# Stage A of batch 1 in the first FFN group, W_out cast on GpSimd, and Y of batch 0 two slots sooner: a Fourier filter with a squared-ReLU FFN on one Trainium2 core

## The chip, the cores and the metric

One core of a Trainium2 chip. The metric is device time in microseconds (us) of one execution; a median of several executions is quoted. TensorE is the matmul engine, VectorE, ScalarE and GpSimd the others, SyncE issues the DMAs. In the profile they are PE (its weight loads PEld), DVE, ACT, POOL and SP.

## The reference

```python
X = np.fft.rfft(x, axis=1)                  # x: 8 x 3008 x 256
Y = X * (filt_r + 1j * filt_i)[None]
y = np.fft.irfft(Y, n=3008, axis=1)
h = np.maximum(y.reshape(24064, 256) @ w_in, 0.0)      # d_ff = 2048
return (h * h @ w_out).astype(np.float32)
```

The FFT is factored: stage A (sums over 47 rows), a re-layout through DRAM (u written as dU, read back as ut), stage B, the product with the filter, stage P, a second re-layout (ze to dZ to zt), and stage Y, which makes the input yt of the FFN. Everything runs as fp16 matmuls.

## The kernel before

The FFN runs in groups of 512 tokens, eight *slots* each. A slot holds one first-layer unit of the group, one second-layer unit of the group before, and pieces of the FFT of a later batch:

```python
for s in range((NG + 1) * SLOTS):
    g, k = divmod(s, SLOTS)
    if g < NG:
        ffn_g1(g, k)            # 4 matmuls + Relu on ScalarE
    run(work, s, 0)             # FFT pieces, place 0
    if g > 0:
        ffn_g2(g - 1, k)        # 8 matmuls
    run(work, s, 1)             # FFT pieces, place 1
    if g > 0:
        ffn_out(g - 1, k)
    if g < NG:
        ffn_sq(g, k)            # square of h on VectorE
```

Batch 0 is transformed ahead of slot 0, as are three quarters of stage A of batch 1. The first group therefore has no second layer beside it. The end of that prologue, and the plan of batch 1 (its slot numbers are those of the loop):

```python
    read_z(0, 0)
    load_wout(0)
    read_z(0, 1)
    load_wout(1)
    for c in (0, 2, 1):
        chunk_a(1, c)           # stage A of batch 1, three of four chunks
    for c in (0, 2, 1):
        write_u(1, c)
    for n in range(4):
        unit_y(0, n)
    prologue[0] = False
    for c in range(2, 4):
        read_z(0, c)            # third and fourth zt tile of batch 0
...
            for n in range(4, 16):
                put(n if n < 8 else n + 2 if n < 12 else 2 * n - 7, n % 2, unit_y, 0, n)
            for k in range(4):
                put((4, 5, 7, 7)[k], 1, cast_wout, k, nc.vector)
        t0 = 2 if b == 1 else 6
        for a in range(12 if b == 1 else 0, 16):
            put(t0 + a // 2, a % 2, unit_a, b, a)
```

Stage A and stage Y units share two PSUM buffers (`psF`). The fp32 W_out lies in a buffer of the ring of h (`h2`), so the first Relu of group 1 has to wait for the last cast of W_out. Y units with odd n are evicted by VectorE in the first group, those with even n by ScalarE.

## Time and profile before

| | |
|---|---|
| time, first three runs | 793.39, 793.43, 793.74 us |
| profiled execution | span 791.9 us, granted clock 1.0 |
| TensorE busy | 778.9 us, 98% |
| Relu of slot 0 to Relu of slot 14 | 50.96 to 73.45: **22.49 us** |

The last row is my yardstick. One row of ScalarE's timeline (start, duration, engine, line, operation, operands, then the idle time before it and what ended it):

```profile
73.45 1.02 ACT L566 ACTIVATE h<-psH 128x1024 f16<-128x1024 f32 x1 [0.89 <-PE psH L562]
```

The rest of the profile before stands in the prediction.

### The profile page before, as it was taken

To read this page: it belongs to the slowest core of one execution; us is meant where nothing else is said; L and a number is where in the kernel's file an instruction comes from. 1 tells how busy PE (TensorE), PEld (TensorE's weight loads), DVE (VectorE), ACT (ScalarE), POOL (GpSimd) and SP (SyncE) were. 2 spreads that over 40 slices of the span, in tenths; PEclk is the share of its full clock that TensorE was granted. 3 is DMA by queue.
4 is the path that set the end of the run, shared out by engine and by line. 5 is a ranking of instruction groups with operands and counts; after the bars stand their busy time and mean duration, and the time that the engine had idled before them with its cause. 6 is when DMAs were issued, how large, how long until landed. Compare 5 with 4: busy or idle time off the path is not lost.

```text
span 791.9 us, 14822 instructions
## 1 busy us (share of the span) xinstructions
PE 778.9 (98%) x6102; PEld 552.5 (70%) x6102; DVE 550.3 (69%) x897; ACT 557.4 (70%) x711; POOL 23.6 (3%) x36
## 2 busy tenths in 40 slices
PE   8989999999999999999999999999999999999998
PEld 5746667667676777867777676776767677676666
DVE  6866994579755897559965699556995579553342
ACT  3976776777777777767776777676777777776664
POOL 3800000000000000000000000000000000000000
PEclk9999999999999999999999999999999999999999
DMA  9994554346814557154562555424563332611111
GB/s 363 368 260 153 146 157 111 93 135 167 205 42 112 167 155 180 48 173 135 132 167 65 163 147 155 112 80 148 159 180 86 97 133 66 147 40 41 41 41 54
DMA packets 88571, 107.32 MB, mean 136 GB/s; under 512 B 6336, under 2 KB 79040, under 8 KB 84288
## 3 DMA queue, kind: packets, MB, share of 16 engines
q1 hardware_dynamic: 88296, 106.19, 46.5%
q8 instruction: 48, 0.79, 0.4%
q10 hardware_dynamic: 144, 0.18, 0.1%
q14 instruction: 19, 0.16, 0.1%
q0 software_dynamic: 64, 0.00, 0.0%
HBM read 58.12 MB, written 48.23 MB: 134 GB/s over the span
## 4 chain that ended last, share of the span: by engine, by line
PE 89%; DVE 6%; DMA 3%; ACT 1%; SPq 0%; issue 0%; DVEq 0%; ACTq 0%
PE psO L579 40%; PE psH L562 38%; PE psA L361 3%; PE psY L532 2%; PE psB L445 2%; DMA f<-in_filt_i_dram 2%; PE psP L496 2%; DVE prod L453 2%; DVE h L570 1%; DMA wout<-in_moe_w_out_dram 1%; PE psf L287 1%; PE psf L290 1%; DVE yf L467 0%; ACT sF L298 0%; DVE yf L461 0%; ACT h L566 0%
## 5 line engine op out<-in xcount | busy, mean ns | idle before, releaser
L566 ACT ACTIVATE h<-psH 128x1024 f16<-128x1024 f32 x376 | 384.9, 1024 | 189.3 <-PE psH L562 186.7
L579 PE MATMUL psO<-sWout,h 128*128 128x256 f16 x3008 | 388.9, 272 | 0.6 <-DVE h L570 0.6
L562 PE MATMUL psH<-yt,sWin 128*128 128x512 f16 (+7 forms) x1728 | 386.9, 351 | 1.6 <-DVE yt L541 0.7
L579 PEld LDWEIGHTS <-h 128*128 128x128 f16 x3008 | 290.6, 98 | 79.1 <-DVE h L570 0.9
L570 DVE TENSOR_TENSOR h<-h 128x1024 f16<-128x1024 f16 x376 | 252.6, 685 | 104.7 <-ACT h L566 104.5
L562 PEld LDWEIGHTS <-sWin 128*128 128x128 f16 x1728 | 159.5, 98 | 101.7 <-issue 3.3
L453 DVE TENSOR_TENSOR prod<-psB,sF 128x1024 f16<-128x1024 f32 x84 | 102.3, 1218 | 2.8 <-PE psB L445 2.8
L541 DVE CAST yt<-psY 128x376 f16<-128x376 f32 x62 | 34.0, 549 | 59.4 <-PE psY L532 59.4
L367 DVE CAST u<-psA 96x512 f16<-96x512 f32 x50 | 34.3, 687 | 47.3 <-PE psA L361 45.1
L498 ACT CAST ze<-psP 128x512 f16<-128x512 f32 x84 | 49.1, 585 | 17.2 <-PE psP L496 14.7
L590 ACT COPY ost<-psO 128x512 f32<-128x512 f32 (+1 forms) x96 | 55.8, 581 | 6.8 <-PE psO L579 5.3
L532 PE MATMUL psY<-sC,zt 112*128 112x94 f16 x512 | 42.4, 205 | 1.4 <-DMA zt<-dZ 1.4
L532 PEld LDWEIGHTS <-zt 112*128 112x128 f16 x512 | 35.1, 98 | 11.6 <-issue 1.6
L467 DVE TENSOR_TENSOR yf<-prod,yf 128x512 f16<-128x512 f16 x84 | 35.7, 425 | 2.9
L361 PE MATMUL psA<-x,sC 94*96 94x512 f16 x96 | 36.6, 382 | 0.0
L445 PE MATMUL psB<-ut,sSB 128*128 128x256 f16 x192 | 36.5, 273 | 0.0
L496 PE MATMUL psP<-yf,sSP 128*128 128x256 f16 x168 | 32.1, 272 | 0.5 <-DVE prod L453 0.3
L539 ACT CAST yt<-psY 128x376 f16<-128x376 f32 x66 | 30.9, 468 | 2.0 <-issue 1.7
L445 PEld LDWEIGHTS <-sSB 128*128 128x128 f16 x192 | 18.5, 98 | 19.5
L340 DVE CAST x<-x 94x2048 f16<-94x2048 f32 x24 | 29.2, 1216 | 0.0
L365 ACT CAST u<-psA 96x512 f16<-96x512 f32 x50 | 28.6, 572 | 0.0
L460 DVE COPY yf<-prod 64x512 f16<-64x512 f16 x84 | 24.3, 289 | 2.9
(65 smaller groups left out, 253.2 us busy)
## 6 DMA issues: line engine op xcount, KB each, us to landing
x<-in_x_dram SPq DMA_DIRECT2D x20, 768.0 KB
zt<-dZ SPq DMA_DIRECT2D x64, 192.0 KB
dU<-u SPq DMA_DIRECT2D x28, 384.0 KB
dZ<-ze SPq DMA_DIRECT2D x28, 384.0 KB
out_dram<-ost SPq DMA_DIRECT2D x66, 128.0 KB
out_dram<-ost SPq DMA_DIRECT2D x31, 256.0 KB
ut<-dU SPq DMA_DIRECT2D x7, 1024.0 KB
xw<-in_x_dram SPq DMA_DIRECT2D x6, 1024.0 KB
```

Source lines behind the costliest of these rows:

```text
L361: nc.tensor.matmul(ps[0:96, :], sSA, x16s[(b, c)][:, m, :], start=True, stop=True)
L445: nc.tensor.matmul(ps[:, i * D:(i + 1) * D], sSB[:, 2 * p + i, :], uts[b][:, 2 * p + i, :], start=True, stop=True)
L453: nc.vector.tensor_mul(out=prod, in0=ps.rearrange("p (a d) -> p a d", d=D).unsqueeze(1).to_broadcast([128, 2, 2, D]), in1=sF[:, :, 2 * p:2 ...
L467: nc.vector.tensor_add(out=yf, in0=prod[:, 0], in1=yf)
L496: nc.tensor.matmul(ps[:, i * D:(i + 1) * D], sSP[:, 2 * p + i, :], yf[:, i, :], start=True, stop=True)
L498: nc.scalar.copy(out=zes[(b, c)][:, 2 * i6:2 * i6 + 2, :], in_=ps.rearrange("p (a d) -> p a d", d=D))
L532: nc.tensor.matmul(ps[:, 94 * jj:94 * jj + 94], zt[:, 4 * (g % 2) + jj, dt * 128:(dt + 1) * 128], sSY, start=True, stop=True)
L562: nc.tensor.matmul(ps[:, i, o:o + n], sWin[:, dt, jt * 128:(jt + 1) * 128], yts[b][:, dt, r:r + n], start=(dt == 0), stop=(dt == 1))
L566: nc.scalar.activation(out=h2[:, 2 * s:2 * s + 2, :], in_=ps, func=AF.Relu)
L570: nc.vector.tensor_mul(out=v, in0=v, in1=v)
L579: nc.tensor.matmul(pso[g][:, t % 2, :], h2s[g][:, jt, t * 128:(t + 1) * 128], sWout[:, jt, :], start=(jt == 0), stop=(jt == NJT - 1))
L590: nc.scalar.copy(out=ost[:, h0:h0 + step, :], in_=pso[g][:, h0:h0 + step, :])
```

## The change

The intent: TensorE idles in group 0, so stage A can move there out of the full slots 8 and 9. Its u cannot take a u buffer (the three are still being written out), so it takes one of x. VectorE evicts it, and to make room there W_out is cast on GpSimd. Y of batch 0 follows two slots sooner.

```diff
         if i == 0:
-            us[(b, c)] = p_u.tile([96, 8, D], F16, tag="u", name=f"u_{b}_{c}")
+            pool, tag = (p_x16, "x16") if b == 1 else (p_u, "u")
+            us[(b, c)] = pool.tile([96, 8, D], F16, tag=tag, name=f"u_{b}_{c}")
...
-        if a % 2 == 0:
+        if a % 2 == 0 and b > 1:
             nc.scalar.copy(out=o, in_=pv)
...
-                put(n if n < 8 else n + 2 if n < 12 else 2 * n - 7, n % 2, unit_y, 0, n)
+                put(n if n < 12 else 2 * n - 7, n % 2, unit_y, 0, n)
             for k in range(4):
-                put((4, 5, 7, 7)[k], 1, cast_wout, k, nc.vector)
-        t0 = 2 if b == 1 else 6
+                put((1, 2, 4, 5)[k], 1, cast_wout, k, nc.gpsimd)
+        t0 = 6
         for a in range(12 if b == 1 else 0, 16):
-            put(t0 + a // 2, a % 2, unit_a, b, a)
+            put(a - 11 if b == 1 else t0 + a // 2, a % 2, unit_a, b, a)
```

## The prediction

> **What bounds the kernel now.** I read the page first: busy shares, then the chain that ended last.
>
> ```profile
> PE 778.9 (98%) x6102; PEld 552.5 (70%) x6102; DVE 550.3 (69%) x897; ACT 557.4 (70%) x711; POOL 23.6 (3%) x36
> PE 89%; DVE 6%; DMA 3%; ACT 1%; SPq 0%; issue 0%; DVEq 0%; ACTq 0%
> ```
>
> TensorE sets the time, and its work is the same after the change: the same matmuls in another order. Only TensorE's idle time can be won or lost, 791.9 - 778.9 = 13 us in all. The change touches the first FFN group (slots 0 to 7, about 51 to 61 us) and slots 8 to 13, so I next read the timeline of each engine there. TensorE:
>
> ```profile
> 57.60 1.02 PE L562 MATMUL psH<-yt,sWin 128*128 128x512 f16 x4
> 58.46 0.33 PE L532 MATMUL psY<-sC,zt 112*128 112x94 f16 x4
> 58.88 0.38 PE L562 MATMUL psH<-yt,sWin 128*128 128x512 f16 x1
> 59.76 0.81 PE L562 MATMUL psH<-yt,sWin 128*128 128x512 f16 x3 [0.50 <-DVE yt L541]
> 60.40 0.38 PE L356 MATMUL psA<-xw,sC 128*96 128x512 f16 x1
> ```
>
> A first-layer unit (4 matmuls, L562) takes 0.87 us of issue, yet slots 6 and 7 start 1.29 us apart: the group has no second layer yet, and TensorE waits for buffers that ScalarE and VectorE empty. The unit of slot 8 waits for the last Y eviction (L541). The stage A unit after it, at 60.40, belongs to what the change moves. ScalarE and VectorE:
>
> ```profile
> 50.96 1.94 ACT L566 ACTIVATE h<-psH 128x1024 f16<-128x1024 f32 x2 [1.31 <-DMA wout<-in_moe_w_out_dram]
> 58.67 1.08 ACT L566 ACTIVATE h<-psH 128x1024 f16<-128x1024 f32 x1
> 60.98 1.02 ACT L566 ACTIVATE h<-psH 128x1024 f16<-128x1024 f32 x1 [1.23 <-DMA zt<-dZ]
> ...
> 57.96 1.28 DVE L570 TENSOR_TENSOR h<-h 128x1024 f16<-128x1024 f16 x2
> 59.16 0.54 DVE L541 CAST yt<-psY 128x376 f16<-128x376 f32 x1
> 59.62 1.28 DVE L333 CAST sWout<-wout 128x1024 f16<-128x1024 f32 x2
> ```
>
> Eight Relus start from 50.96 to 58.67. A Relu lasts 1.02 us and the next can start 0.92 later (1.94 - 1.02); VectorE's squares and casts come 0.60 apart (1.28 - 0.68). The Relu at 60.98 is named as waiting for a DMA, but the last W_out cast ended at 59.62 + 1.28 = 60.90: the h buffer of group 1 is the one that holds the fp32 W_out, so I put this wait down to the cast.
>
> From 60.40 TensorE has no gap until 80.75. Thereafter VectorE is nearly continuous too, with 0.2 to 0.6 us gaps on TensorE. So a gain or loss made before slot 8 should be carried unchanged to the end.
>
> **What the Trainium skill says.** "SBUF — State Buffer", section "Who interferes with whom": VectorE and GpSimd share one port pair; a VectorE cast in a 2-port mode, or a tensor_tensor with two SBUF inputs, and a GpSimd instruction that reads SBUF exclude each other for the whole instruction. The trace agrees for casts:
>
> ```profile
> 20.49 1.04 POOL L222 CAST f<-f 128x1024 f16<-128x1024 f32 x1 [2.37 <-DMA f<-in_filt_i_dram]
> 20.56 1.51 DVE L222 CAST f<-f 128x1024 f16<-128x1024 f32 x1 [0.26 <-DMA f<-in_filt_i_dram]
> ```
>
> VectorE's cast usually takes 0.68 us; here it ended 0.54 after GpSimd's. For the squares (L570, two SBUF inputs) no overlap with GpSimd occurs in this trace, so that half of the statement is unseen here. "DMA: Bandwidth & Descriptors", section "Queues, rings and completion order": each DMA engine consumes a ring's descriptors in order. That fits the completion records in the trace (16 per transfer): the transfers of the SyncE queue land in issue order.
>
> **The change, part by part.** The order of instructions on each engine shows what moves.
>
> 1. Stage A units 12 to 15 (8 matmuls, 0.435 us of issue each unit: 60.40 to 60.84) leave slots 8 and 9, where TensorE is full. Removed there: 4 x 0.435 = 1.74 us. They go to slots 1 to 4. They can because their u takes a free x buffer instead of waiting for the write of an older u.
>
> 2. VectorE in group 0 loses four W_out casts and gains four u casts (L367), each 0.60 apart: a draw, but earlier. ScalarE loses two u casts in slots 8 and 9; that is off the path.
>
> 3. Cost in group 0. I write starts from the Relu at 50.96, with these rules, all read from the rows: TensorE can reuse a buffer 0.06 us after its eviction ends; an eviction can follow 0.19 to 0.20 us after the issue end of its matmuls; a Relu after a Y cast is 0.36 later than that cast. The same rules reproduce the kernel before (Relu 5 at 56.51, second-layer Y eviction at 59.16, 59.76 for the wait). For the new order, without any port lock:
>
> - Unit 12 at 51.58 fits a gap of TensorE; first layer 2 stays at 52.04. Unit 13 at 52.91 pushes layer 3 to 53.34; unit 14 at 54.21 pushes layer 4 to 54.64.
> - VectorE: square 0 52.02, u12 52.62, square 1 53.22, u13 53.82, square 2 54.42, u14 55.02 to 55.71. Unit 15 shares a PSUM buffer with unit 14 and waits: 55.77. Layer 5 then at 56.20 instead of 55.20.
> - Relu 5 57.26, Relu 6 58.38, y6 to 59.80, square 6 59.43, y7 60.03 to 60.57. Slot 8's first layer: second matmul 60.63, issue end 60.63 + 3 x 0.217 = 61.28, instead of 60.40.
>
> So the group ends 0.88 us later, and the gain is 1.74 - 0.88 = 0.86 us.
>
> 4. Y of batch 0, units 8 to 11, now in slots 8 to 11: no work added. But unit 8 stands in TensorE's order before the first second-layer unit, and it reads the third zt tile, which comes from a queue that is issued as follows:
>
> ```profile
> 47.10 7.71 SPq L344 DMA_DIRECT2D dU<-u  x3
> 54.86 3.23 SPq L514 DMA_DIRECT2D zt<-dZ  x4
> 65.70 0.32 SPq L344 DMA_DIRECT2D dU<-u  x1
> 68.99 0.82 SPq L436 DMA_DIRECT2D ut<-dU  x2
> ```
>
> By the completion records the halves of that tile land at 60.55 and 62.22. Before, unit 8 ran at 65.62. After, it would come up at 61.28 and wait to about 62.22 + 0.14 = 62.36 (the first Y of all ran 0.14 after its landing). That is 1.08 us, so 0.86 turns into a loss of 0.22 us.
>
> 5. W_out on GpSimd: four casts at about 1.0 us (35.15 to 39.14 has four such in 3.99). The halves of W_out land at 51.59 and 56.35, so two casts run about 51.6 to 54 and two about 56.4 to 59. If the squares are shut out as the skill says, and VectorE and GpSimd take turns: square 0 52.68, u12 53.28, square 1 54.25, u13 54.85, square 2 55.45, u14 56.05, square 3 57.40, u15 58.00, square 4 59.00, y5 59.60, square 5 60.07, square 6 60.67, y7 61.27 to 61.82. Slot 8's first layer ends about 62.5, 2.1 us later than before instead of 0.88. Unit 8's tile has then landed, so the two costs lie beside each other: 2.1 - 1.74 = about 0.4 us lost.
>
> 6. u of chunk 3 is written about 58 to 59 instead of 65.70, so the ut reads go out before 66 and land well ahead of stage B in slot 14. Nothing waited there before (psB at 73.25 follows without a gap), so it gains nothing.
>
> **Rivals.** (a) *Clean gain*: no lock on squares and the zt tile in time, -0.86 us, 792.6. For: the tile's last completion is one engine's (15 of 16 were done at 61.28), so it may come earlier. Against: that alone still leaves unit 8 at the edge, and the lock seen on casts. (b) *The zt wait takes over*: +0.2 us, 793.65. For: the landing times; the DMA traffic before them is unchanged. (c) *The port lock makes VectorE the bound of group 0*: +0.4, 793.85; up to +1.0 if two GpSimd casts run back to back before square 0, 794.4. For: the pair of rows above; VectorE has only about 1.9 us of slack in the group's 10 (12 instructions at 0.60 and two at 0.47 fill the rest). (d) *Contention later*: the earlier ut read collides with output writes; the queue is idle from 63 to 66, so I give it little.
>
> **Range and chances.** I weigh (a) at 0.2, (b) at 0.25, (c) at 0.5 and something unforeseen at 0.05: 793.6 us. The range 792.4 to 794.8 spans the clean gain and the bad form of the lock, with 0.3 for variation between runs. All rivals lie within 0.2% of the time before; 2% would be 15.9 us, more than TensorE's whole idle time.
>
> **What would show it.** Right if stage A units stand in slots 1 to 4 with unit 15 waiting for VectorE; if the first second-layer unit starts at 61.5 to 63 instead of 60.84 and four stage A units no longer follow; if squares beside GpSimd casts last 1.0 to 1.6 us; if unit 8 waits for zt or for a late first layer. Wrong if the squares stay at 0.69 us beside GpSimd and the Y unit runs with no gap (then 792.6), or if the distance from slot 8 to slot 14 or to the end changes by more than the moved units, which would mean a bound later that I have not seen.

## The result, and the profile after

794.08 us median of four runs (793.53, 793.64, 794.52, 794.58) against 793.59 before (four runs). The ratio is 1.0003, with a 95% interval of 0.9985 to 1.002: the same. A ratio here is the mean time of one kernel's runs over that of the other's of the same rounds, so not quite the ratio of the medians quoted. The two longer runs of the four had a granted clock of 0.998 and 0.999, the other two 1.0; those two lie within 0.3 us of the first three runs before.

The yardstick says the same: Relu 0 at 50.93, Relu 14 as follows, 22.49 us apart, to the hundredth what it was.

```profile
73.42 1.02 ACT L567 ACTIVATE h<-psH 128x1024 f16<-128x1024 f32 x1 [0.71 <-PE psH L563]
```

(Lines from 352 on are one higher than before.) Yet much moved in between. TensorE's timeline in the first group:

```profile
56.35 0.38 PE L357 MATMUL psA<-xw,sC 128*96 128x512 f16 x1 [0.56 <-DVE u L368]
56.78 1.03 PE L563 MATMUL psH<-yt,sWin 128*128 128x512 f16 x4
...
61.14 0.81 PE L563 MATMUL psH<-yt,sWin 128*128 128x512 f16 x3 [0.45 <-DVE yt L542]
62.12 0.33 PE L533 MATMUL psY<-sC,zt 112*128 112x94 f16 x4 [0.17 <-DMA zt<-dZ]
62.28 1.04 PE L580 MATMUL psO<-sWout,h 128*128 128x256 f16 x8
```

The fourth stage A unit stands for 0.56 us on u of the unit before it, which pushes the first layer of slot 5 behind it. Slot 8's first layer waits for the last Y eviction as before, now until 61.14 instead of 59.76. The issue of its three matmuls ends at 61.14 + 3 x 0.217 = 61.79, and the Y unit starts at 62.12: 0.33 us of standing, put down to zt. The last completion records of that tile are at 61.98. VectorE and GpSimd beside it:

```profile
51.98 1.07 DVE L571 TENSOR_TENSOR h<-h 128x1024 f16<-128x1024 f16 x1 [2.00 <-DMA zt<-dZ]
53.58 0.92 DVE L571 TENSOR_TENSOR h<-h 128x1024 f16<-128x1024 f16 x1
55.02 0.67 DVE L571 TENSOR_TENSOR h<-h 128x1024 f16<-128x1024 f16 x1
58.90 0.88 DVE L571 TENSOR_TENSOR h<-h 128x1024 f16<-128x1024 f16 x1
...
51.47 2.48 POOL L333 CAST sWout<-wout 128x1024 f16<-128x1024 f32 x2 [12.26 <-DMA wout<-in_moe_w_out_dram]
56.36 2.88 POOL L333 CAST sWout<-wout 128x1024 f16<-128x1024 f32 x2 [2.40 <-DMA wout<-in_moe_w_out_dram]
```

Four squares that meet a GpSimd cast last 0.75 (the one at 57.59, not shown) to 1.07 us; the one at 55.02, between the two pairs of casts, 0.67. Each of the four ends 0.53 to 0.54 us after the end of a GpSimd cast (the first cast ends at 52.52, the square at 53.05). GpSimd's first cast lasts 1.04 us, the three others 1.44 to 1.50. From slot 8 to slot 14 the four stage A units (1.74 us) are gone, and the later end of slot 8's first layer (61.79 - 60.40 = 1.39) and the wait for zt (0.33) make 1.72: the gain is used up almost exactly.

### The profile page after: what moved, and what is told of

Read it like the earlier page. It is cut to its first block, busy times and chain, and to the rows that moved or that the text cites. A ratio compares the mean times of both kernels' runs of the same rounds, so it can differ in the third digit from the quotient of the medians.

```text
span 791.9 us, 14814 instructions
## 1 busy us (share of the span) xinstructions
PE 778.8 (98%) x6102; PEld 552.5 (70%) x6102; DVE 550.2 (69%) x895; ACT 557.1 (70%) x709; POOL 29.1 (4%) x40
## 4 chain that ended last, share of the span: by engine, by line
PE 91%; DMA 4%; DVE 3%; ACT 1%; SPq 1%; issue 0%; DVEq 0%; ACTq 0%
PE psO L580 40%; PE psH L563 39%; PE psA L362 3%; PE psY L533 3%; PE psB L446 2%; PE psP L497 2%; DMA f<-in_filt_i_dram 2%; DMA zt<-dZ 1%; DVE prod L454 1%; DVE h L571 1%; PE psf L287 1%; PE psf L290 1%; ACT sF L298 0%; DVE yf L468 0%; DVE prods L454 0%; DMA dZ<-ze 0%
## 5 line engine op out<-in xcount | busy, mean ns | idle before, releaser
L542 DVE CAST yt<-psY 128x376 f16<-128x376 f32 x62 | 34.1, 549 | 59.6 <-PE psY L533 59.6
```

## The experiments

All on one chip, which also ran the kernel before beside them. *Yardstick* is Relu 0 to Relu 14 of the profiled run (before: 22.49; after: 22.49); times are medians. The edits are against the kernel named.

| run | Relu 0, Relu 14 | yardstick | against before | time (runs) | ratio, 95% interval |
|---|---|---|---|---|---|
| only_y | 51.40, 75.41 | 24.01 | +1.52 (clock dip inside) | 795.67 (4) | 1.002, 1.0006 to 1.0035 |
| only_pool | 50.81, 73.92 | 23.11 | +0.62 | 794.42 (4) | 1.0008, 0.9992 to 1.0025 |
| only_a | 50.64, 72.51 | 21.87 | -0.62 | 793.20 (4) | 0.9993, 0.9979 to 1.0008 |
| y_late | 50.78, 72.80 | 22.02 | -0.47 | 793.49 (4) | 0.9994, 0.9979 to 1.0008 |
| zt_first | 51.20, 74.52 | 23.32 | +0.83 | 794.41 (4) | 0.9999, 0.9982 to 1.0016 |
| zt_first_write_only | 52.73, 74.34 | 21.61 | -0.88 | 794.47 (4) | 1.0002, 0.9988 to 1.0017 |
| pro_a | 51.04, 71.90 | 20.86 | -1.63 | 792.08 (4) | 0.9975, 0.996 to 0.999 |
| pro_a_pool | 51.04, 72.41 | 21.37 | -1.12 | 792.76 (4) | 0.9983, 0.9966 to 0.9999 |
| pro_a_y | 51.13, 78.27 | 27.14 | +4.65 (dip inside) | 797.12 (4) | 1.0033, 1.001 to 1.0056 |
| pro_a_zt_y | 51.01, 72.01 | 21.00 | -1.49 | 792.15 (4) | 0.9975, 0.9955 to 0.9995 |
| pro_a_y7 | 50.83, 71.50 | 20.67 | -1.82 | 791.63 (6) | 0.9969, 0.9952 to 0.9985 |
| pro_a_zt_y7 | 51.12, 71.26 | 20.14 | -2.35 | 791.50 (5) | 0.9966, 0.9952 to 0.998 |

My theory after the result: stage A in the gaps of group 0 gains; the shared port of VectorE and GpSimd takes back one part, TensorE standing for zt the other. The rivals: the zt wait is absorbed by slack, or the moved stage A itself gains nothing.

**A first thing the runs showed: two clocks.** Of the 17 runs of the kernel before that stand beside these, eleven have a granted clock of 0.999 or 1.0 and 793.16 to 793.89 us, six 0.998 and 794.89 to 795.17. The profiled run of only_y is one of the second kind. The windows view (busy time of PE, PEld, DVE, ACT and POOL with the number of instructions, then the granted clock, DMA share and GB/s) of 50 to 53 us, of only_y and then of before:

```profile
50.00:53.00 3.00, 3.00 (x8) 1.12 (x8) 0.55 (x1) 1.02 (x1) 0.00 (x0) 0.52 1.08 222
```

```profile
50.00:53.00 3.00, 2.70 (x13) 1.11 (x12) 0.77 (x3) 1.94 (x2) 0.00 (x0) 1.00 1.06 231
```

The clock record of only_y is 0.5 from 50.09 for 3.41 us. Ahead of this point TensorE stands 1.1 us for the first zt tile (47.0 to 48.2; 1.4 us in before, 46.8 to 48.3), with small matmuls around. The Trainium skill, "TensorE: Matmul & The Clock Gate", section "What's actually happening", says that a monitor halves the clock after an idle window of about 3.4 us, 3413 ns long and free-running. The length fits; that a gap of 1.1 us can be enough is what these traces add. The gap alone does not decide it: before with 1.4 us and zt_first with 1.4 us show no dip in their profiled runs. What does stays open.

### only_y

The kernel before with this line of the change alone:

```diff
-                put(n if n < 8 else n + 2 if n < 12 else 2 * n - 7, n % 2, unit_y, 0, n)
+                put(n if n < 12 else 2 * n - 7, n % 2, unit_y, 0, n)
```

> The kernel before with Y units 8 to 11 alone moved two slots sooner. Theory 1 (TensorE stands at Y unit 8 until the third zt tile has landed, and this is on the path): unit 8 comes up at about 60.4 and starts at about 62.1, so the Relu of slot 14 moves from 73.45 to about 75.1 and the time grows by about 1.7 us, to 795.2. Rival (the wait is absorbed by slack in slots 8 to 13): the Relu of slot 14 stays within 0.3 us of 73.45.

All four runs had the clock of a dip (0.997 or 0.998). In the profiled one it had shifted group 0 by 1.15 us when slot 8's first layer ended at 61.56. The Y unit then stood until 62.09 for a tile that lands at its own time (last record at 61.96). So only the rest was left to wait, and against the dipped runs of before (794.89 to 795.17) the kernel is 0.5 to 0.8 us slower, not 1.7. The direction is as expected; the size could not be told here, because of the dip. pro_a_y below repeats it without one ahead of it.

### y_late

The changed kernel with that line undone.

> The changed kernel with Y units 8 to 11 back at slots 10 to 13. Theory 1: no wait for zt; the first second-layer unit starts at about 61.8 instead of 62.28, and the Relu of slot 14 comes at about 73.1 instead of 73.42, 0.3 us gained. Rival (group 0 alone decides, the zt wait costs nothing): slot 14 within 0.05 us of the changed kernel.

```profile
60.86 0.81 PE L563 MATMUL psH<-yt,sWin 128*128 128x512 f16 x3 [0.45 <-DVE yt L542]
61.50 1.03 PE L580 MATMUL psO<-sWout,h 128*128 128x256 f16 x8
```

No gap between the first and the second layer of slot 8, and the yardstick is 0.47 us shorter than the changed kernel's. Of this 0.33 is the gap. The other 0.14 is group 0 ending sooner: here the first half of W_out landed at 51.86 instead of 51.42, and square 0 got away unhindered (0.69 us). Theory held, its size a little larger.

### zt_first and zt_first_write_only

zt_first is the changed kernel with the reads of two tiles ahead of the u writes:

```diff
+    for c in range(2, 4):
+        read_z(0, c)
     for c in (0, 2, 1):
         write_u(1, c)
...
-    for c in range(2, 4):
-        read_z(0, c)
```

zt_first_write_only also lets GpSimd write where it cast, so its output is wrong:

```diff
-        eng.tensor_copy(out=sWout[:, c, :], in_=w32s[2][:, c, :])
+        eng.memset(w32s[2][:, c, :], 0.0)
```

(sWout is set to zero in the prologue.)

> The changed kernel with the reads of the third and fourth zt tile issued ahead of the three u writes. Theory 1: the zt tiles land before 60, Y unit 8 runs with no gap behind the first-layer unit of slot 8 at about 61.8, and the Relu of slot 14 comes at about 73.1, as where Y is late. Rival: another wait takes the place (u write or ut read late, or the W_out half later), and slot 14 stays at 73.4 or grows.

> As zt_first, but GpSimd only writes in the place of the four W_out casts (a memset of the fp32 W_out tile, the same 1024 columns of fp32, at the same points and after the same landings); the output is wrong on purpose. Theory of the shared read port: squares of group 0 all last 0.69 us instead of 0.75 to 1.07, the fourth stage A unit waits less, and slot 8's first layer ends about 0.5 us sooner than in zt_first (61.3 against 61.8). Rival (GpSimd instructions of any kind hold squares up, or the squares are long for another reason): squares of 0.75 to 1.1 us as before.

In the profiled run zt_first lost: the yardstick is 0.83 us over before. It is the slowest of four runs; another took 793.25 us at the full clock, and with a ratio of 0.9999 the order is not shown to lose as a rule. Its rows of VectorE and GpSimd, then those of zt_first_write_only:

```profile
59.11 2.96 DVE L571 TENSOR_TENSOR h<-h 128x1024 f16<-128x1024 f16 x2 [0.18 <-ACT h L567]
61.99 0.53 DVE L542 CAST yt<-psY 128x376 f16<-128x376 f32 x1
59.04 2.48 POOL L333 CAST sWout<-wout 128x1024 f16<-128x1024 f32 x2 [3.68 <-DMA wout<-in_moe_w_out_dram]
```

```profile
60.08 0.69 DVE L571 TENSOR_TENSOR h<-h 128x1024 f16<-128x1024 f16 x1 [0.18 <-ACT h L567]
59.21 1.85 POOL L333 MEMSET wout<- 128x1024 f32 x2 [4.19 <-DMA wout<-in_moe_w_out_dram]
```

In this trace the rival of zt_first came true. The zt wait is gone (unit 8 runs at 63.22 without a gap, its tile landed at 60.69, not before 60), but the second half of W_out had its last completion record at 58.98 (the other 15 by 56.93; before: 56.35), so both casts ran from 59.04 to 61.52, and squares 5 and 6 took 2.96 us instead of 1.28 and held the last Y eviction to 61.99. The four profiled runs with the reads first have that last record at 58.5 to 59.2, all others at 57.2 or sooner: it comes with the order, as far as one trace of each tells. In zt_first the transfers behind it trail too (third zt tile: 15 records by 58.92, the last at 60.69). Why one of the 16 records trails stays open.

In the write-only run a square runs at 0.69 us right beside GpSimd's memsets (59.21 to 61.06), as do all others of the group (0.68 to 0.69). GpSimd being busy is not what slows a square; the cast is, and what the memset leaves out of it is the read of SBUF (it also writes another tile, which no run varies alone). That run's yardstick is 21.61, 0.88 us under before: stage A moved, W_out off VectorE, no lock and no zt wait. It is 1.71 us under zt_first, whose W_out landed as late. (The clock dip in this run, from 49.00 to 52.42, lies ahead of Relu 0.)

### only_pool and only_a

The two other parts of the change, each alone in the kernel before.

> The kernel before with the four W_out casts alone put on GpSimd (slots 1, 2, 4, 5). Theory: VectorE of group 0 loses 4 x 0.60 us of casts and gains about 0.9 us of longer squares, but the last Y eviction hangs on square 6, which hangs on ScalarE; so slot 8's first layer ends at about 60.4 as before, and slot 14 stays within 0.3 us of 73.45. Rival (the casts were what held the group up): slot 14 comes 1 us or more sooner.

> The kernel before with stage A alone moved (slots 1 to 4, u in a buffer of x, evicted by VectorE); W_out stays on VectorE and Y stays late. Theory: VectorE has 16 instructions at 0.60 and two at 0.47 in group 0, 10.5 us, so it becomes the group's bound; slot 8's first layer ends at about 63 instead of 60.4 and slot 14 comes about 0.9 us later than 73.45 (74.3); the cast on GpSimd is then what makes room, worth 1.2 to 1.5 us against the run with Y late. Rival: the port lock costs as much as the casts, and slot 14 comes as in the run with Y late, 0.5 us sooner than before.

Both theories fell, and the rival of only_a came true. By the yardstick only_pool lost 0.62 us, only_a gained 0.62. VectorE in only_pool, TensorE in only_pool, and VectorE in only_a:

```profile
57.43 2.29 DVE L570 TENSOR_TENSOR h<-h 128x1024 f16<-128x1024 f16 x2
59.64 0.53 DVE L541 CAST yt<-psY 128x376 f16<-128x376 f32 x1
```

```profile
60.22 0.81 PE L562 MATMUL psH<-yt,sWin 128*128 128x512 f16 x3 [1.12 <-DVE yt L541]
```

```profile
58.77 1.28 DVE L571 TENSOR_TENSOR h<-h 128x1024 f16<-128x1024 f16 x2
59.98 0.54 DVE L542 CAST yt<-psY 128x376 f16<-128x376 f32 x1
60.43 1.28 DVE L333 CAST sWout<-wout 128x1024 f16<-128x1024 f32 x2
```

On VectorE the third and fourth W_out cast stand *behind* the last Y eviction, on which TensorE waits. There they cost nothing that the yardstick shows. On GpSimd they run as soon as the second half of W_out has landed, 56.3 to 59.2, beside squares 5 and 6, which stand *ahead* of that eviction; the two squares take 2.29 us instead of 1.28. The engine was relieved of work that did not count, and the work that counted was slowed. In only_a I had counted all 16 instructions of VectorE ahead of the eviction; three of them, two casts and square 7, stand behind it.

### pro_a and pro_a_pool

TensorE's gap ahead of group 0 can take the last quarter of stage A itself. pro_a, against before:

```diff
-        u = p_u.tile([96, 8, D], F16, tag="u", name=f"u_{b}_{c}")
+        pool, tag = (p_x16, "x16") if c == 3 else (p_u, "u")
+        u = pool.tile([96, 8, D], F16, tag=tag, name=f"u_{b}_{c}")
...
-        for a in range(12 if b == 1 else 0, 16):
+        for a in range(16 if b == 1 else 0, 16):
...
-    for c in (0, 2, 1):
+    for c in (0, 2, 1, 3):
         chunk_a(1, c)
-    for c in (0, 2, 1):
+    for c in (0, 2, 1, 3):
         write_u(1, c)
```

pro_a_pool has W_out on GpSimd too.

> The kernel before with the last quarter of stage A of batch 1 done ahead of the first FFN group, in the gap of TensorE from 46.9 to 48.3 us, its u in a buffer of x; W_out on VectorE and Y late as before. Theory: stage A leaves slots 8 and 9 (1.74 us) and costs group 0 nothing, so slot 14 comes about 1.6 us sooner (71.9) and the time is about 791.9. The clock record halves for 3.4 us at about 50 in the runs that are 1.0 us slow (granted clock 0.998); with that gap filled it should not, and no run should show 0.998. Rival (PSUM banks or the u writes hold up the first FFN units): slot 14 gains less than 0.8 us.

> As pro_a, with W_out cast on GpSimd. Theory: as for W_out alone, no more than 0.3 us either way against pro_a. Rival (in this order VectorE's casts are what ends last in group 0): 0.5 us or more sooner than pro_a.

pro_a: 1.63 us off the yardstick, of the 1.74 us of stage A. All four runs lie at 792.00 to 792.29 with clock 1.0. None of the 23 runs of the pro_a kernels other than pro_a_y is at 0.998, where 6 of 17 of before are: filling the gap removed the dip too. (Of the difference in the mean times, 0.25%, part is that.) pro_a_pool gives back 0.51 us, by the same lock as in only_pool: more than I had expected, and against the rival.

### pro_a_y and pro_a_zt_y

> pro_a with Y units 8 to 11 two slots sooner, nothing else (no clock dip is expected, so this tells the zt wait apart cleanly). Theory: in pro_a the third zt tile lands at 63.9 by the completion records, and unit 8 comes up at 60.5, so TensorE stands for about 3.5 us and the Relu of slot 14 moves from 71.90 to about 75.4, the time to about 795.5. Rival (the wait is absorbed): within 0.3 us of pro_a.

> pro_a_y with the reads of the third and fourth zt tile issued ahead of the u writes. Theory: the tile lands before 60.5 and unit 8 does not wait; slot 14 back at 71.9 within 0.2 us, time about 792.1, so that Y sooner by itself brings nothing and costs nothing. Rival (the place of Y, not the tile, costs): still more than 0.5 us behind pro_a.

pro_a_y, TensorE's timeline:

```profile
64.29 0.47 PE L533 MATMUL psY<-sC,zt 112*128 112x94 f16 x4 [3.56 <-DMA zt<-dZ]
64.55 1.70 PE L580 MATMUL psO<-sWout,h 128*128 128x256 f16 x7
```

3.56 us of standing, as expected, for a tile whose last record is at 64.15. That wait brings a dip of its own: the clock is 0.5 from 63.00 for 6.83 us (seven second-layer matmuls take 1.70 us here, eight 1.04 at the full clock), so the loss against pro_a is 6.3 us in this run and 5.0 by the medians. With the reads first, pro_a_zt_y is back within 0.14 us of pro_a on the yardstick and 0.07 by the medians. So Y two slots sooner gains nothing, and what it costs is the tile's landing alone.

### pro_a_y7 and pro_a_zt_y7

pro_a_y7 puts Y unit 7 into slot 6, ahead of square 6 on VectorE; pro_a_zt_y7 has the zt reads first as well.

```diff
-                put(n if n < 8 else n + 2 if n < 12 else 2 * n - 7, n % 2, unit_y, 0, n)
+                put(6 if n == 7 else n if n < 8 else n + 2 if n < 12 else 2 * n - 7, n % 2, unit_y, 0, n)
```

> pro_a with Y unit 7 in slot 6 instead of 7, so that VectorE evicts it ahead of square 6. Theory (the last Y eviction behind square 6 is what ends last in group 0): slot 8's first layer runs without its 0.50 us wait and ends at about 59.9 instead of 60.48; slot 14 at about 71.3, time about 791.5. Rival (the W_out casts, which hold the first Relu of group 1 to 61.0, become the bound): slot 14 gains less than 0.2 us against pro_a.

> pro_a_y7 with the reads of the third and fourth zt tile issued ahead of the u writes; Y units 8 to 11 at slots 10 to 13 as before. Theory: in pro_a_y7 unit 8 of slot 10 again met the landing (TensorE idle 0.37 us at 63.67); with the reads sooner that gap goes, slot 14 comes about 0.4 us sooner than 71.50 at the same start of the first Relu, and the time is about 791.2. Rival (moving the reads delays the second half of W_out or ut, and that ends last): no gain, or a loss.

pro_a_y7, VectorE and TensorE, then pro_a_zt_y7:

```profile
58.42 0.54 DVE L542 CAST yt<-psY 128x376 f16<-128x376 f32 x1
58.75 1.08 PE L563 MATMUL psH<-yt,sWin 128*128 128x512 f16 x4 [0.20 <-ACT yt L540]
63.67 0.33 PE L533 MATMUL psY<-sC,zt 112*128 112x94 f16 x4 [0.37 <-DMA zt<-dZ]
```

```profile
62.57 1.03 PE L563 MATMUL psH<-yt,sWin 128*128 128x512 f16 x4
63.43 0.33 PE L533 MATMUL psY<-sC,zt 112*128 112x94 f16 x4
```

The last Y eviction starts 0.8 us sooner than in pro_a (59.24), and slot 8's first layer runs in one piece. But TensorE now comes early enough to meet the zt landing even in slot 10, so only 0.19 us of the expected 0.6 arrives. With the reads first it all arrives: 20.14, 2.35 us under before, and 791.50 us against 793.68, ratio 0.9966 (0.9952 to 0.998). The interval lies below 1, and the slowest of its five runs (791.52) is 2 us under the fastest of the changed kernel (793.53, not run beside it). Its output is correct. A part of the ratio is the dip that no longer comes.

## Why the prediction was right or wrong

The time was right: 793.6 predicted, 794.08 measured, within 792.4 to 794.8. Some of that is luck: the lock was made too large and the zt wait too small, and the two errors partly cancel (point 4). The range was wide besides: the medians of before and of six of the twelve experiments lie in it. The 0.48 us between 793.6 and 794.08 come from the two longer runs, of which no trace was kept. By its steps:

1. *A clean gain of 0.86 us from stage A.* Right in kind and size: zt_first_write_only, where neither lock nor tile interferes, gained 0.88, and its last Y eviction ends 9.61 us after Relu 0, as the prediction has it (60.57 - 50.96). Unit 15 waited for VectorE as written.
2. *The zt wait, up to 1.08 us.* The mechanism was right (y_late, pro_a_y). In the changed kernel it was a gap of 0.33 us, because the lock had already delayed what stands ahead of it; the text had let the two lie beside each other, with nothing left of this one. The unit started at 62.12 against 62.36 predicted.
3. *The port lock, and a group that ends 2.1 us later.* The kind was right, with squares of 0.75 to 1.07 us (1.0 to 1.6 predicted). The size was not: the group ended 1.39 us later by the trace (61.79 against 60.40). I had taken square 3 to be shut out until 57.40; it began at 56.22, before the second pair of casts at 56.36, and square 4 was over at 58.34 instead of about 59.6. The prediction let a held-up square begin afresh when the cast ends; held-up squares end 0.53 to 0.54 us after it, as the prediction's own pair of casts had shown (0.54).
4. *The sum.* Predicted +0.2 to +0.4 us; the yardstick shows 0.00. In the trace of the changed kernel, counted from Relu 0, slot 8's first layer ends 1.42 us later than before: 0.88 is the clean cost, which leaves 0.54 for the lock (1.22 predicted, 2.1 - 0.88). The zt wait adds 0.33 (nothing predicted beside the lock), and 1.42 + 0.33 stands against the 1.74 us moved. Between runs the split is +0.41 for the lock (y_late against zt_first_write_only) and +0.47 for the sooner Y (after against y_late). All of these are of single traces and move by some 0.15 us with when W_out lands.
5. *VectorE in group 0: a draw, with 1.9 us of slack.* This reading failed: it counted twelve instructions as if all had to be done before the group ends, but two W_out casts and square 7 stand behind the last Y eviction. What it missed is where the casts stood. only_pool and only_a show that the cast on GpSimd is a loss by itself: 0.62 us in the kernel before, and 0.15 us with stage A moved (only_a against y_late), which is no more than W_out's landing can move.
6. *The ut read sooner gains nothing.* Right: it went out at 65.22 instead of 68.99, and no gap stood there before or after.
7. *0.3 us for variation between runs.* Too little: the clock dip makes 1 us. (And 792.6 - 0.3 is 792.3, not 792.4.)

The rivals fell as follows: clean gain, not in this kernel but shown by a run; zt wait and lock, both true, and together as large as the gain; later contention, not seen: the distances are constant from slot 14 on.

## What to carry to other kernels

Before work is moved off a busy engine, look at what stands behind it in that engine's order: work behind the last thing anybody waits for is free where it is, and on another engine it can run sooner and get in the way. A unit that is pulled forward must find its data landed: the completion times of the transfers say so before the kernel is run. And a stretch where TensorE idles is best filled where it is idle by itself, which here kept its clock up as well.

## What the Trainium skill lacked or had wrong

- "SBUF — State Buffer", "Who interferes with whom": nothing wrong was found. Its two-input case, unseen in the prediction's trace, is borne out: squares beside GpSimd casts take 0.75 to 1.52 us, beside GpSimd memsets 0.69. What it lacks is the time that a blocked instruction still needs: here a held-up square ends 0.53 to 0.55 us after the cast (0.69 us alone).
- "TensorE: Matmul & The Clock Gate", "HAM oscillation — how this bites in real kernels": its rule is no idle gap over about 3.4 us, too lax for this case. A gap of 1.1 us (47.0 to 48.2 in only_y), with small matmuls around it, came before a dip of 3.41 us; 6 of 17 runs of before had the clock of such a dip and cost 1 us more, and none of 23 once the gap was filled. The page has a kernel with short idles that lose the clock, but no size for them. In pro_a_y a gap of 3.56 us brought a dip of 6.83 us.
- "DMA: Bandwidth & Descriptors", "Why a DMA increments its semaphore by 16 and not by 1": the engines of one transfer finish independently, it says; how far the last can trail is not given. Here it was 2 us (56.93 and 58.98, the second half of W_out), which decides when a waiting cast starts. The cause is open.
